# Soft-capped attention feeding a slot mixture of experts: casting loads, a second exponential tile per batch on VectorE, and three small jobs moved to the thin steps

## The chip, the cores and the metric

The kernel runs on one core of a Trainium2 chip. The metric is device time in microseconds (us), given as the median of several runs of the same compiled kernel. A profile is one further execution recorded by the hardware profiler, and its span is about 2 us shorter than the device time. The engines are PE (TensorE, matmuls), ACT (ScalarE), DVE (VectorE), POOL (GpSimd) and SP (which here only issues transfers). PEclk is the clock that the hardware granted to PE, as a fraction of full speed.

Ratios are computed as the mean time of one kernel's fast runs over that of the other's fast runs recorded with them, so they are not quite the ratio of the medians quoted beside them. A run is called slow when it is over 1.5% above the fastest run of the same kernel. The program runs on this one core alone.

## The reference, cut to what matters

```python
def _attn_ref(q, k, v, cap):                     # q, k, v: (8, 12, 448, 64)
    scores = scale * np.matmul(q, k.transpose(0, 1, 3, 2))
    scores = cap * np.tanh(scores / cap)          # cap = 30
    attn = np.exp(scores - max); attn /= attn.sum(-1)
    return np.matmul(attn, v)

def _moe_ref(x, phi, w1, w2):                    # x: (3584, 768), 32 slots, 8 experts
    logits = x @ phi
    d = softmax over tokens of logits; slot_input = d.T @ x
    slot_out = relu(slot_input @ w1) @ w2         # per expert
    c = softmax over slots of logits
    return c @ slot_out
```

Every score needs one tanh and one exponential. That is 8 x 12 x 448 x 448 scores, twice, and it is the bulk of the work.

## The kernel before

Attention is cut into 56 chunks of six score tiles (128 x 448 each), seven chunks per batch. I call one chunk's turn in the program a step and number the steps of a batch 0 to 6. In each step ACT does two tanh instructions (from PSUM, three tiles each) and one exponential over six tiles in place. Step 2 of each batch has no value products, and I call it the thin step. One tile per batch is taken from ACT: DVE computes its exponential by a polynomial, in three parts.

```python
def exp_chunk(j):
    exp_part(j, 1 if j in shared else 0, CH)       # ACT: six tiles, or five
shared = [j for j in range(NCH - 2) if j % 7 == 3 and j > 7] if cap < 80 else []

def poly_exp(j, part):                              # DVE: the sixth
    if part == 0:   ...                             # three tensor_scalar
    elif part == 1: ...                             # two scalar_tensor_tensor on SBUF operands
    else:           ...                             # two more, the last writes the tile

def cast(nm, Q):                                    # q or k of four heads: f32 to bf16, reordered
    dve.tensor_copy(t.rearrange("p c (h d) -> p h c d", h=2),
                    raws.pop((nm, Q)).rearrange("p h (c d) -> p h c d", d=DH))
    if Q > 1: load(nm, Q + 1)

def transp(nm, Q):
    for c in range(NT):
        pe.transpose(ps[:, c, :], src[:, c, :], ident)
    dve.tensor_copy(t, ps)

def e_transp(b):     # transposes of the combine weights, in the single buffer "T" of PSUM
    ps = psT.tile([P, 512], BF16, name="eps", tag="T")
    for g in (3, 0, 1, 2):
        pe.transpose(ps[:, GOFF[g]:GOFF[g] + P], e4s[b][:, g, :], ident)
    dve.tensor_copy(ET4..., ps...)
# e_norm(b): 4 matmuls "zps", then DVE adds "zacc";  e_sums: 7 matmuls "wps", then DVE "winv"
# x_transp(pr): 4 transposes "xps", then DVE copies "xT";  logits: 8 matmuls "lps", then DVE "lg"
# all of these use the one buffer "T" in turn

at(j + 1, "d", spare, 34 if b == 0 else 10)         # warm-up matmuls that compute nothing of use
...
at(j + 12, "d", e_transp, b)                        # step 5
at(j + 13, "d", e_norm, b)                          # step 6
at(j + 14, "d", e_sums, b // 2)                     # step 0, every other batch
for j in shared:
    for dj, slot, part in ((0, "a", 0), (0, "c", 1), (0, "d", 2)):
        at(j + dj, slot, poly_exp, j, part)
```

The slots of a step run in program order: tanh and exponential, value products of the first half, "a", scores, "b", value products of the second half, "c", scores, "d". In the timelines below each engine starts its instructions in this order.

The softmax here doesn't subtract the row's maximum and nothing guards it: scores larger than these inputs give would overflow.

## Time and profile before

| | before |
|---|---|
| time, median (range) | 318.18 us (317.34 to 319.43) |
| busy: PE / ACT / DVE / POOL | 269.4 / 281.3 / 193.7 / 106.5 us of a span of 314.8 |
| one batch, from one small exponential (L366) to the next | 32.56 us |
| ACT idle before tanh (L278) | 0.9 us in all |
| mean granted clock | 0.983 |

Read it like this: a busy share is an average, so it does not say what sets the time. The chain of waits and the idle column of ACT do. ACT hardly waits between about 7 and 268 us (busy 261.1 of 261.2 us), so in that stretch its work alone is the time. The prediction shows the lines.

### The profile page before, as it was taken

How to read it: one execution, taken by the hardware profiler on the slowest of the kernel's cores; microseconds unless marked ns; L12 is line 12 of the kernel's file. 1: busy time of each engine (PE TensorE's matmuls, PEld its weight loads, DVE VectorE, ACT ScalarE, POOL GpSimd, SP SyncE). 2: the span in 40 equal slices, each digit the busy share in tenths (PEclk: the TensorE clock that was granted, in tenths of full speed). 3: DMA queues.
4: the chain of work that ended last, by engine and by line, in shares of the span. 5: the costliest groups of instructions: out<-in, count | busy, mean ns of one | idle time of the engine just before them, and what ended most of it. 6: DMA issues, size and time to landing. Idle time of an engine off the chain costs nothing.

```text
span 314.8 us, 8844 instructions
## 1 busy us (share of the span) xinstructions
PE 269.4 (86%) x3804; PEld 191.0 (61%) x3804; DVE 193.7 (62%) x473; ACT 281.3 (89%) x208; POOL 106.5 (34%) x134
## 2 busy tenths in 40 slices
PE   7899898899889998898889989898889998998720
PEld 6667665667666665666666666666666677743400
DVE  3636565766586659575867587657766574327840
ACT  4999999999999999999999999999999999326730
POOL 2464342523543452354245416441732130200000
PEclk9999999999999999999999999999999999999985
DMA  8899999799999999999999999999999807898997
GB/s 223 267 234 238 291 244 269 159 231 256 235 210 231 266 237 207 254 220 266 194 225 269 221 264 190 242 235 266 209 232 254 214 14 207 290 393 301 389 411 314
DMA packets 57479, 77.68 MB, mean 247 GB/s; under 512 B 3809, under 2 KB 53601, under 8 KB 57441
## 3 DMA queue, kind: packets, MB, share of 16 engines
q0 software_dynamic: 30480, 25.22, 52.1%
q1 hardware_dynamic: 26672, 51.68, 48.1%
q8 instruction: 29, 0.48, 0.6%
q10 hardware_dynamic: 288, 0.23, 0.2%
q14 instruction: 10, 0.07, 0.1%
HBM read 91.32 MB, written 18.87 MB: 350 GB/s over the span
## 4 chain that ended last, share of the span: by engine, by line
ACT 67%; PE 20%; DVE 5%; issue 3%; DMA 2%; DVEq 0%; ACTq 0%
ACT ex L278 33%; ACT ex L282 32%; PE pv L318 5%; PE sc L269 3%; PE so_ps L676 2%; PE junk L506 2%; PE hp L649 2%; ACT ob L754 1%; PE op L702 1%; DMA kraw<-in_k_dram 1%; DVE xq L329 1%; PE op L745 1%; PE xps L344 1%; DMA out_dram<-obh 1%; DVE ob L752 1%
## 5 line engine op out<-in xcount | busy, mean ns | idle before, releaser
L278 ACT ACTIVATE ex<-sc 128x1344 bf16<-128x1344 f32 (+1 forms) x113 | 162.3, 1693 | 0.9 <-PE sc L269 0.8
L282 ACT ACTIVATE ex<-ex 128x2688 bf16<-128x2688 bf16 (+4 forms) x58 | 159.2, 2779 | 0.1
L318 PEld LDWEIGHTS <-ex 128*128 128x128 bf16 x1344 | 78.7, 97 | 21.5 <-DVE xq L329 17.8
L318 PE MATMUL pv<-vbd,ex 128*128 128x130 bf16 x1274 | 88.6, 220 | 2.6 <-ACT ex L282 0.7
L269 PE MATMUL sc<-qT,kT 64*64 64x448 bf16 x672 | 78.6, 358 | 8.2 <-ACT ex L278 7.9
L247 POOL CAST vbd<-vraw 64x896 bf16<-64x896 f32 x23 | 21.5, 936 | 103.6 <-PE pv L318 65.3
L269 PEld LDWEIGHTS <-kT 64*64 64x64 bf16 x672 | 27.3, 105 | 25.3 <-issue 7.5
L329 DVE TENSOR_TENSOR xq<-pv,rec 128x256 bf16<-128x256 f32 x91 | 38.6, 424 | 3.1
L328 DVE RECIPROCAL rec<-pv 128x4 f32<-128x4 f32 x91 | 16.5, 181 | 32.1 <-PE pv L318 31.2
L506 PEld LDWEIGHTS <-ones 128*128 128x128 bf16 x470 | 28.6, 100 | 11.6 <-DVE xq L329 8.0
L372 POOL COPY e<-E 128x512 bf16<-128x512 bf16 x9 | 7.2, 795 | 81.5 <-ACT E L366 49.6
L506 PE MATMUL junk<-ones 128*128 128x128 bf16 x433 | 31.4, 219 | 2.5 <-DVE xq L329 1.6
L239 DVE COPY kT<-kps 128x896 bf16<-128x896 bf16 x23 | 14.4, 625 | 24.6 <-PE kps L237 24.4
L109 POOL DMA_DIRECT2D w1b<-in_moe_w_dram x32 | 25.2, 791 | 0.0
L248 POOL CAST vbd<-vraw 64x896 bf16<-64x896 f32 x23 | 23.7, 1029 | 1.3
L346 DVE COPY xT<-xps 128x512 bf16<-128x512 bf16 x47 | 19.5, 415 | 3.2 <-PE xps L344 3.0
L344 PE MATMUL xps<-ident,xq 128*128 128x128 bf16 x188 | 18.1, 218 | 0.2 <-DVE zacc L383 0.2
L239 DVE COPY qT<-qps 128x896 bf16<-128x896 bf16 x23 | 14.2, 616 | 5.2 <-PE qps L237 5.2
L226 DVE CAST kbf<-kraw 128x896 bf16<-128x896 f32 x22 | 16.0, 728 | 1.3 <-DMA kraw<-in_k_dram 1.3
L237 PE MATMUL kps<-ident,kbf 128*128 128x128 bf16 x161 | 12.8, 219 | 4.2 <-DVE slacc L418 2.2
L237 PE MATMUL qps<-ident,qbf 128*128 128x128 bf16 x161 | 12.8, 219 | 3.2 <-DVE lg L360 2.7
L237 PEld LDWEIGHTS <-kbf 128*128 128x128 bf16 x161 | 10.0, 97 | 9.0 <-issue 8.3
(113 smaller groups left out, 255.5 us busy)
## 6 DMA issues: line engine op xcount, KB each, us to landing
w1b<-in_moe_w_dram POOLq DMA_DIRECT2D x32, 384.0 KB, 10.2
vraw<-in_v_dram SPq DMA_DIRECT2D x23, 448.0 KB, 6.6
qraw<-in_q_dram SPq DMA_DIRECT2D x22, 448.0 KB, 7.8
kraw<-in_k_dram SPq DMA_DIRECT2D x22, 448.0 KB, 6.0
w2d<-in_moe_w_dram POOLq DMA_DIRECT2D x20, 384.0 KB, 9.2
w2t<-w2d SPq DMA_DIRECT2D x20, 384.0 KB, 5.9
out_dram<-ob SPq DMA_DIRECT2D x8, 768.0 KB, 7.3
w2b<-in_moe_w_dram POOLq DMA_DIRECT2D x12, 384.0 KB, 9.9
```

What stands on the lines that cost most here:

```text
L109: pool.dma_start(out=w1b[e][:, js, fs], in_=w1r[:, e, js, fs])
L237: pe.transpose(ps[:, c, :], src[:, c, :], ident)
L239: dve.tensor_copy(t, ps)
L247: pool.tensor_copy(t[0:HP, :, :, 0:DH], raw[0:HP])
L248: pool.tensor_copy(t[HP:P, :, :, DH + 1:VW - 1], raw[HP:P])
L269: pe.matmul(sc[cs, u, 0:S], qkT["k", Q][r, c, cs], qkT["q", Q][r, :, cs], start=True, stop=True)
L278: act.activation(exs[j][:, half * CS + u0:half * CS + u1, :], sc[:, u0:u1, 0:S], ACT.Tanh, scale=qk_scale / cap)
L282: act.activation(exs[j][:, u0:u1, :], exs[j][:, u0:u1, :], ACT.Exp, scale=cap)
L318: pe.matmul(pvs[pr, half][:, n, 0:VW], exs[j][:, u, GOFF[g]:GOFF[g] + P], vbds[Q % 2][:, h, c, :], start=(c == 0 and n == 0), stop=(c == N ...
L329: dve.tensor_tensor(xq[Q][:, 2 * half:2 * half + 2, h * P:(h + 1) * P] .rearrange("p g (i d) -> p g i d", i=2), pv[:, :, :, 0:DH], rec.to_ ...
L344: pe.transpose(ps[:, g, :], xq[Q][:, g, h * P:(h + 1) * P], ident)
L506: pe.matmul(junk if home is None else home, ones, ones, start=True, stop=True)
```

## The change

The intent: give ACT less to do by moving a second tile per batch to DVE. To make room on DVE, q and k are cast to bf16 by the transfers, and the transfers are issued by POOL. The reordering that DVE's cast did on the way is given up, so each key or query transpose becomes two of 64 columns. To make room on PE in the dense steps, three small jobs go to steps 1 and 2, and warm-up matmuls are cut.

```diff
-    def cast(nm, Q):            # DVE cast of each q and k
+    def load(nm, Q):            # bf16 tiles, two buffers
+            (sp if nm == "v" else pool).dma_start(out=t, in_=quad_ap(nm, Q))
...
+            for h in range(2):
+                pe.transpose(ps[h * HP:h * HP + HP, c, :], src[:, h, c * DH:(c + 1) * DH], ident)
...
-    shared = [j for j in range(NCH - 2) if j % 7 == 3 and j > 7] if cap < 80 else []
+    shared = [j for j in range(NCH - 2) if j % 7 in (1, 3) and j > 7] if cap < 80 else []
...
-        at(j + 1, "d", spare, 34 if b == 0 else 10)
-        at(j + 2, "d" if b == 0 else "a", spare, 4 if b == 0 else 14)
+        at(j + 1, "d", spare, 34 if b == 0 else 6)
+        at(j + 2, "d" if b == 0 else "a", spare, 4 if b == 0 else 12)
...
-        at(j + 3, "d", spare, 10)
+        at(j + 3, "d", spare, 10 if b == 0 else 4)
...
-                at(j + 12, "d", e_transp, b)
-                at(j + 13, "d", e_norm, b)
+                at(j + 15, "d", e_transp, b)        # step 1
+                at(j + 16, "d", e_norm, b)          # step 2
             if b % 2:
-                at(j + 14, "d", e_sums, b // 2)
+                at(j + 16, "d", e_sums, b // 2)     # step 2
     for j in shared:
-        for dj, slot, part in ((0, "a", 0), (0, "c", 1), (0, "d", 2)):
-            at(j + dj, slot, poly_exp, j, part)
+        for slot, part in (("a", 0), ("c", 1)):
+            at(j, slot, poly_exp, j, part)
+        at(j + 1, "b" if j % 7 == 1 else "a", poly_exp, j, 2)
```

Cut: the first loads with their tiles, and the loads' new slots.

More of the change, by code (lines that the diff above doesn't have):

```diff
@@ L90 @@
     w1b = [wts.tile([P, NJ, F], BF16, name=f"w1b{e}", tag="w1", bufs=E)
-           for e in range(E - 1)]
+           for e in range(E - 2)]
     w2b = wts.tile([P, R2, D], BF16, name="w2b")
@@ L129 @@
     ld = att.enter_context(tc.tile_pool(name="ld", bufs=1))
-    cst = att.enter_context(tc.tile_pool(name="cst", bufs=1))
     ldv = att.enter_context(tc.tile_pool(name="ldv", bufs=1))
@@ L158, in raw_tile @@
     def raw_tile(nm):
-        return (ldv if nm == "v" else ld).tile([P, 2, S], F32, name=nm + "raw",
-                                               tag=nm + "raw")
+        if nm == "v":
+            return ldv.tile([P, 2, S], F32, name="vraw", tag="vraw")
+        return ld.tile([P, 2, S], BF16, name=nm + "b", tag=nm + "raw", bufs=2)
     def load(nm, Q):
@@ L164, in load @@
             t = raw_tile(nm)
-            sp.dma_start(out=t, in_=quad_ap(nm, Q))
+            (sp if nm == "v" else pool).dma_start(out=t, in_=quad_ap(nm, Q))
             raws[nm, Q] = t
     def load_first():
-        for nm in "qkv":
-            raws[nm, 0] = raw_tile(nm)
-        kc = raws["k", 0].rearrange("p h (c d) -> p h c d", d=DH)
+        for nm in "qk":
+            raws[nm, 0] = [ld.tile([P, S], F32, name=f"{nm}raw{h}", tag=nm + "raw", bufs=2)
+                           for h in range(2)]
+        raws["v", 0] = raw_tile("v")
+        kc = raws["k", 0][0].rearrange("p (c d) -> p c d", d=DH)
         kin = quad_ap("k", 0, 0).rearrange("p (c d) -> p c d", d=DH)
-        sp.dma_start(out=raws["q", 0][:, 0, :], in_=quad_ap("q", 0, 0))
+        sp.dma_start(out=raws["q", 0][0], in_=quad_ap("q", 0, 0))
         for c0, c1 in ((0, CS), (CS, NT)):
-            act.dma_start(out=kc[:, 0, c0:c1, :], in_=kin[:, c0:c1, :])
+            act.dma_start(out=kc[:, c0:c1, :], in_=kin[:, c0:c1, :])
         for nm in "kq":
-            sp.dma_start(out=raws[nm, 0][:, 1, :], in_=quad_ap(nm, 0, 1))
+            sp.dma_start(out=raws[nm, 0][1], in_=quad_ap(nm, 0, 1))
         t = wts.tile([P, 3, 2, S], F32, name="raw1", tag="w1", bufs=E)
+        t01 = wts.tile([P, 2, 2, NT, P], BF16, name="casts", tag="w1", bufs=E)
         for n, nm in enumerate("kqv"):
             raws[nm, 1] = t[:, n, :, :]
+            if nm != "v":
+                for Q in range(2):
+                    casts[nm, Q] = t01[:, n, Q, :, :]
             if nm == "v":
@@ L192, in first_pieces @@
                 copy(casts[nm, 0][:, c0:c1, cols],
-                     raws[nm, 0][:, h, c0 * DH:c1 * DH].rearrange("p (c d) -> p c d", d=DH))
+                     raws[nm, 0][h][:, c0 * DH:c1 * DH].rearrange("p (c d) -> p c d", d=DH))
             elif stage == "turn":
@@ L202, in first_half @@
             if h == 0:
-                casts[nm, 0] = cst.tile([P, NT, P], BF16, name=nm + "bf", tag=nm + "bf")
                 qkT[nm, 0] = qk.tile([P, NT, P], BF16, name=nm + "T", tag=nm + "T")
@@ L222, in first_half, with cast @@
                 load(nm, 2)
-    def cast(nm, Q):
-        t = cst.tile([P, NT, P], BF16, name=nm + "bf", tag=nm + "bf")
-        dve.tensor_copy(t.rearrange("p c (h d) -> p h c d", h=2),
-                        raws.pop((nm, Q)).rearrange("p h (c d) -> p h c d", d=DH))
-        casts[nm, Q] = t
-        if Q > 1:
-            load(nm, Q + 1)
+    def cast(nm):
+        dve.tensor_copy(casts[nm, 1].rearrange("p c (h d) -> p h c d", h=2),
+                        raws.pop((nm, 1)).rearrange("p h (c d) -> p h c d", d=DH))
     def transp(nm, Q):
-        src = casts.pop((nm, Q))
+        src = casts.pop((nm, Q)) if Q == 1 else raws.pop((nm, Q))
         home = (psV, "pv") if (nm, Q) == ("k", 1) else (psT, "T")
@@ L236, in transp @@
         for c in range(NT):
-            pe.transpose(ps[:, c, :], src[:, c, :], ident)
+            if Q == 1:
+                pe.transpose(ps[:, c, :], src[:, c, :], ident)
+                continue
+            for h in range(2):
+                pe.transpose(ps[h * HP:h * HP + HP, c, :], src[:, h, c * DH:(c + 1) * DH], ident)
         t = qk.tile([P, NT, P], BF16, name=nm + "T", tag=nm + "T")
@@ L441, in quad_in @@
         if 0 < Q < NQ:
-            at(*cast_k, cast, "k", Q)
-            at(*cast_q, cast, "q", Q)
+            for nm, when in (("k", cast_k), ("q", cast_q)):
+                at(*when, *((cast, nm) if Q == 1 else (load, nm, Q + 1)))
             at(*k_in, transp, "k", Q)
@@ L453 @@
             quad_in(3 * b + 1, (j - 1, "b"), (j, "a"), (j - 1, "d"), (j, "c"), (j + 1, "d"))
-        quad_in(3 * b + 2, (j + 1, "c"), (j + 2, "c"), (j + 2, "b"), (j + 2, "d"),
+        quad_in(3 * b + 2, (j, "d"), (j + 1, "c"), (j + 2, "b"), (j + 2, "d"),
                 (j + 4, "d"))
-        quad_in(3 * b + 3, (j + 4, "a"), (j + 5, "a"), (j + 4, "d"), (j + 5, "c"),
+        quad_in(3 * b + 3, (j + 4, "a"), (j + 5, "a"), (j + 3, "d"), (j + 5, "c"),
                 (j + 6, "d"))
         p = 6 * b
-        at(j + 1, "d", spare, 34 if b == 0 else 10)
-        at(j + 2, "d" if b == 0 else "a", spare, 4 if b == 0 else 14)
+        at(j + 1, "d", spare, 34 if b == 0 else 6)
+        at(j + 2, "d" if b == 0 else "a", spare, 4 if b == 0 else 12)
         if b:
             at(j + 2, "c", spare, 8)
-        at(j + 3, "d", spare, 10)
+        at(j + 3, "d", spare, 10 if b == 0 else 4)
         at(j + 4, "a", x_transp, p)
@@ L476 @@
             if b < B - 2:
-                at(j + 12, "d", e_transp, b)
-            if b < B - 2:
-                at(j + 13, "d", e_norm, b)
+                at(j + 15, "d", e_transp, b)
+                at(j + 16, "d", e_norm, b)
             if b % 2:
-                at(j + 14, "d", e_sums, b // 2)
+                at(j + 16, "d", e_sums, b // 2)
     for j in shared:
-        for dj, slot, part in ((0, "a", 0), (0, "c", 1), (0, "d", 2)):
-            at(j + dj, slot, poly_exp, j, part)
+        for slot, part in (("a", 0), ("c", 1)):
+            at(j, slot, poly_exp, j, part)
+        at(j + 1, "b" if j % 7 == 1 else "a", poly_exp, j, 2)
     for n, job in enumerate(wjobs):
```

## The prediction

> **What bounds the kernel now.** I read the share of each engine first, then the chain that ended last, then the groups by shape, then one steady batch in order of time. From the page, the chain:
>
> ```profile
> ACT 67%; PE 20%; DVE 5%; issue 3%; DMA 2%; DVEq 0%; ACTq 0%
> ```
>
> Two thirds of the span hang on ScalarE (ACT). The groups by shape (busy us, mean ns, then idle time before them) say which instructions, and that nothing holds them up:
>
> ```profile
> L278 ACT ACTIVATE ex<-sc 128x1344 bf16<-128x1344 f32 x111 | 161.1, 1710 | 0.0
> L282 ACT ACTIVATE ex<-ex 128x2688 bf16<-128x2688 bf16 x48 | 137.7, 2869 | 0.1
> ...
> L282 ACT ACTIVATE ex<-ex 128x2240 bf16<-128x2240 bf16 x7 | 18.1, 2579 | 0.0
> ...
> L226 DVE CAST kbf<-kraw 128x896 bf16<-128x896 f32 x22 | 16.0, 728 | 1.3 <-DMA kraw<-in_k_dram 1.3
> L226 DVE CAST qbf<-qraw 128x896 bf16<-128x896 f32 x22 | 14.5, 660 | 0.0
> ```
>
> The tanh (L278) and exponential (L282) instructions overlap, so their means exceed what each adds. The timeline of ACT gives the cost by start times (start us, us, engine, line):
>
> ```profile
> 114.58 2.79 ACT L282 ACTIVATE ex<-ex 128x2688 bf16<-128x2688 bf16 x1
> 116.92 2.82 ACT L278 ACTIVATE ex<-sc 128x1344 bf16<-128x1344 f32 x2
> ...
> 121.59 0.67 ACT L366 ACTIVATE E<-lg 128x128 bf16<-128x128 f32 x1
> ...
> 124.13 2.45 ACT L282 ACTIVATE ex<-ex 128x2240 bf16<-128x2240 bf16 x1
> 126.09 1.67 ACT L278 ACTIVATE ex<-sc 128x1344 bf16<-128x1344 f32 x1
> ```
>
> A full exponential of six tiles takes 116.92 - 114.58 = 2.34 us, one of five tiles (the sixth done by VectorE) 126.09 - 124.13 = 1.96 us. Two tanh take 2.35 us, so a step (one chunk of six tiles) is 4.69 us, and a batch of seven steps runs from 121.59 to the next small exponential at 154.15: 32.56 us, with ACT busy all of it. From 6.8 to about 268 us this engine sets the time; the remaining 47 us (expert layers, output) are other code and the change does not touch them.
>
> TensorE (PE) is a close second. Two batches by windows (busy us and count by engine):
>
> ```profile
> 96.00:128.56 32.56, 29.20 (x425) 21.21 (x423) 22.27 (x56) 32.56 (x24) 13.52 (x17) 1.00 1.06 230
> 128.56:161.12 32.56, 28.96 (x418) 21.12 (x416) 22.01 (x55) 32.56 (x24) 13.29 (x17) 1.00 1.06 225
> ```
>
> PE is idle only some 3.4 us of 32.56, and most of that is round trips to VectorE (DVE) through single buffers, not spare time.
>
> [...] The weight transfers of this kernel do so already: their median from issue to landing is 10.2 us for w1, against 6.0 and 7.8 us for the plain k and q loads.[...] six 448-column score matmuls, two column halves, take 0.57 us[...].
>
> **The change, part by part.**
>
> *Exponential tiles.* Shared chunks were those with j mod 7 = 3, 10 to 52: seven. Those with j mod 7 = 1 from 8 to 50 are added: seven more. ACT loses 7 x 0.373 = 2.6 us. This lies on the path, so the ideal is 318.17 - 2.6 = 315.6 us. DVE gains per tile the seven polynomial instructions, 382 + 394 + 394 + 613 + 626 + 666 + 872 ns = 3.95 us, 27.6 us in all.
>
> *Casts.* 44 casts leave DVE: 22 x 728 + 22 x 660 ns = 30.5 us. DVE's load thus stays near 190 us (62%): the casts pay for the polynomials. They were not on the path, so removing them alone gives nothing.
>
> *Transfers.* 44 loads of 448 KB move from SP's queue to POOL's, landing as bf16. POOL's issue costs about 0.77 us each (row of the weight issues): 34 us more on an engine busy 106 of 315 us, mostly waiting. HBM reads are unchanged. Landing grows from 6 to 8 us towards the 10 us of the weights, but the loads now have two buffers and are issued about 11 to 14 us ahead of their transposes (by my reading of POOL's order: after a value cast at 127.3, for a transpose near 139). I expect them hidden.
>
> *Key and query transposes.* Without the reordering cast, each 128x128 transpose becomes two of 64 columns in the two column halves: 44 x 7 = 308 more matmuls. Before, the first quad did exactly this form:
>
> ```profile
> 7.85 0.55 PE L196 MATMUL ps<-ident,kbf 128*64 128x128 bf16 x7
> 8.24 0.55 PE L196 MATMUL ps<-ident,qbf 128*64 128x128 bf16 x7
> ```
>
> Seven take 8.24 - 7.85 = 0.39 us, 55 ns each, the same as full ones. There all seven were in one half. If two halves run together as the score matmuls do, the extra is near zero; if not, it is 6 x 7 x 55 ns = 2.3 us per batch.[...]
>
> *Fillers and the thin step.* Twelve fewer warm-up matmuls per batch from the second on: 12 x 55 = 0.66 us back. The weights' transposes, normalizer and sums, each with a DVE round trip of 0.2 to 0.5 us, move from the dense steps to those with fewer value products. Key transposes of one quad move one step earlier. This evens PE out.
>
> *Sum for PE per batch.* Free before: about 1 us of waiting for ACT (7.9 us over 7.5 batches), plus 0.66 us of fillers removed, plus about 0.3 us of round trips hidden, less the 0.37 us by which ACT gets shorter: 1.6 us. Needed: 0 to 2.3 us[...]. So in the parallel case ACT stays the bound; in the serial case PE overshoots ACT's new period by 0.7 to 1.3 us per batch, that is 5 to 9 us over seven batches on top of 315.6.
>
> **Rivals.**
> 1. *PE becomes the bound* because the half transposes are serial. For: PE is already 90% busy in a batch, and the second score group of a dense step ends only 0.7 to 0.8 us before ACT needs it (98.62 against 99.4 us). Against: the concurrent score matmuls, and the trimmed fillers, which look balanced by hand. It would make 320 to 325 us.
> 2. *Late loads on POOL's queue.* For: [...]the weights are 768 KB of reading each, and one took 16.0 us to land; POOL also waits up to 6.6 us on value products before it can issue. Against: the lead of 11 to 14 us and unchanged bytes. If each batch lost 0.5 to 1 us: 319 to 323 us.
> 3. *Polynomials in DVE's way*: parts of 1.2, 1.2 and 1.5 us ahead of a reciprocal that frees the single value buffer. For: PE's weight loads waited 17.8 us on that line before. Against: the third part was moved a step later, and casts of 0.6 to 0.7 us leave the same queue. At most a few tenths per batch: 316 to 318 us.
> 4. *More gain than 2.6 us*: nothing speaks for it, as ACT had 1 us of idle time in all and the tail is unchanged. Beyond 314 us would need a faster start or tail.
>
> **How the range follows.** I choose the parallel case with two in three, small stalls of about 0.4 us in all on top of 315.6: 316.0. The serial or late-load cases, one in three, lift the upper end; the spread of the runs before (317.34 to 318.18) sets the lower. Range 314.5 to 320.0 us. Faster by over 2% means under 311.8, which ACT's arithmetic excludes: 0.02. Slower by over 2% means over 324.5[...]: 0.06. Within 2%: 0.92.
>
> **What would show it.** ACT's five-tile exponentials count 14, six-tile ones 41; the batch from one small exponential to the next is 32.2 us; ACT idle before L278 stays under 2 us. The transposes show in pairs: 14 in 0.45 to 0.6 us rather than 0.94. No wait of a transpose on a k or q load. DVE busy near 190 us. I am wrong if ACT waits on score matmuls, PE on these loads, or if the pairs are serial and the batch exceeds 32.6 us.

Some passages of the prediction are cut, at the marks, because they rested on rules or figures that no trace or run of this case shows. The forecast came to 318.17 - 7 x 0.373 = 315.6 us, plus stalls of about 0.4 us, so 316.0 us. The passage that first gave 0.373 us is cut, but the trace before shows the figure: from its start to the next start on ACT a six-tile exponential takes 2.333 us and a five-tile one 1.960 us, by the median. In the sum for PE one term is cut: an estimate of about 0.1 us for each change between groups of different tile shape, 0.6 us per batch. With it PE needed up to 2.3 + 0.6 = 2.9 us against the 1.6 us free, which is the overshoot of 1.3 us per batch, or 9 us in all. Without it the overshoot is at most 0.7 us, or 5 us in all. The 0.06 for slower by over 2% rested on that cut term.

"Do so" of the weight transfers means that they cast while they land and that POOL issues them. That the score matmuls run in pairs is measured in the trace before: the six start two by two, within 0.03 us of each other, most often at 0, 0.21 and 0.40 us, and a group takes 0.57 to 0.76 us. One after another they would take about 1.2 us. That is an estimate from the 55 ns of a 128-column transpose: 6 x 448 / 128 x 55 ns.

## The result and the profile after

The changed kernel takes 335.63 us (333.34 to 337.21, four runs, all fast) against 318.18 us. The ratio is 1.054, with a 95% interval of 1.047 to 1.061. The prediction was 316.0 us with a range of 314.5 to 320.0, and 0.06 for slower by over 2%. It was wrong.

From the page of the changed kernel, the chain that ended last; then, from its groups by shape, ACT's instructions (now at L286 and L290) and the second instruction of the polynomial's second part (L309):

```profile
ACT 48%; PE 31%; DVE 14%; issue 2%; DMA 1%; DVEq 0%; ACTq 0%
```

```profile
L286 ACT ACTIVATE ex<-sc 128x1344 bf16<-128x1344 f32 x111 | 140.4, 1341 | 17.0 <-PE pv L326 13.0 <-PE sc L277 3.9
L290 ACT ACTIVATE ex<-ex 128x2688 bf16<-128x2688 bf16 x41 | 102.5, 2499 | 0.1
L290 ACT ACTIVATE ex<-ex 128x2240 bf16<-128x2240 bf16 x14 | 29.9, 2136 | 0.0
...
L309 DVE SCALAR_TENSOR_TENSOR xp<-xp,xm 128x448 f32<-128x448 f32 x14 | 13.1, 938 | 0.5
```

The 14 exponentials of five tiles are there as planned, but ACT now stands idle 17.0 us before its tanh. Its share of the chain fell from 67% to 48%, and PE's and DVE's rose to 31% and 14%. So ACT got less work and then waited for PE. The releaser "PE pv" (13.0 us of the 17.0) is to be taken as it stands. A tanh writes one of four buffers named ex in turn, and the value products (pv) of the chunk four steps back still read that buffer. At the wait of 2.73 us shown below, the last value product that reads the buffer ends at 124.90 us and the tanh starts at 124.94, while its scores had ended at 124.10.

Where it goes is seen in four batches by windows, each from one small exponential to the next (length, then busy us and count of PE, PEld, DVE, ACT, POOL, then the granted clock, the DMA share and GB/s):

```profile
88.18:121.91 33.73, 30.10 (x439) 21.39 (x440) 20.90 (x55) 32.80 (x23) 18.01 (x22) 0.93 1.08 193
121.91:157.84 35.93, 32.69 (x457) 23.11 (x454) 22.25 (x57) 32.51 (x23) 16.74 (x21) 0.88 1.00 172
157.84:195.83 37.99, 34.11 (x451) 23.76 (x449) 22.90 (x57) 32.62 (x23) 17.63 (x22) 0.81 0.99 166
195.83:231.24 35.41, 31.79 (x465) 22.15 (x464) 22.92 (x60) 32.30 (x23) 17.50 (x22) 0.96 0.98 172
```

The batches are 33.7 to 38.0 us long instead of 32.2, and the granted clock, 1.00 in these batches before, is down to 0.81. The number of matmuls differs little from batch to batch, yet PE's busy time grows, because each takes longer: 68.4 to 75.6 ns of busy time for one, against 29.08 us over 457 = 63.6 ns in a batch of number 2 below, at a clock of 1.00.

One thin step shows the cause. First PE's timeline (start, us, engine, line, what; idle time before it in brackets):

```profile
110.84 0.40 PE L399 MATMUL eps<-ident,e 128*128 128x128 bf16 x4
111.21 0.51 PE L514 MATMUL junk<-ones 128*128 128x128 bf16 x6
113.31 0.38 PE L352 MATMUL xps<-ident,xq 128*128 128x128 bf16 x4 [1.58 <-DVE ET L400]
113.53 1.44 PE L514 MATMUL junk<-ones 128*128 128x128 bf16 x12
114.90 1.33 PE L277 MATMUL sc<-qT,kT 64*64 64x448 bf16 x6
```

Then DVE at the same time:

```profile
111.07 0.61 DVE L308 SCALAR_TENSOR_TENSOR xp<-xm 128x448 f32<-128x448 f32 x1
111.72 1.23 DVE L309 SCALAR_TENSOR_TENSOR xp<-xp,xm 128x448 f32<-128x448 f32 x1
112.88 0.38 DVE L400 COPY ET<-eps 128x448 bf16<-128x448 bf16 x1
```

The weights' transposes (eps) end at 111.24, but the copy that frees the single PSUM buffer starts only at 112.88. It stands in DVE's queue behind the second part of the new tile's polynomial. The x transposes (xps) need that buffer. No matmul that stands after them in the program begins before them, the fillers included, and so PE stands still for 1.58 us. The granted clock (third number from the end) then falls, from 1.00 in the window before these:

```profile
112.00:114.00 2.00, 0.69 (x9) 0.69 (x9) 1.53 (x3) 2.00 (x3) 1.94 (x3) 0.89 1.24 204
114.00:116.00 2.00, 2.00 (x16) 1.05 (x13) 0.15 (x1) 2.00 (x2) 2.00 (x3) 0.50 1.23 228
116.00:118.00 2.00, 2.00 (x29) 1.42 (x28) 0.85 (x2) 1.71 (x2) 0.02 (x1) 0.76 1.13 269
```

The next score group takes 1.33 us where 0.76 was usual, and ACT runs dry for 2.73 us:

```profile
124.94 2.47 ACT L286 ACTIVATE ex<-sc 128x1344 bf16<-128x1344 f32 x2 [2.73 <-PE pv L326]
```

Over the run the x transposes waited 10.9 us in six batches, up to 2.3 us each. Before the change they did not wait for that copy at all; the logits (lps) waited for it 2.9 us in six batches, up to 0.5 us each.

L309 itself takes 1.23 us where its twin in step 3 takes 0.62. All seven in step 1 took 1.23 to 1.26 us, and each overlaps a value cast on POOL that took 1.23 to 1.24 instead of 0.96 us. L309 is so up to 0.63 us longer. The instruction before it (L308, of the same kind) took up to 1.27 us instead of 0.61 in the same places. In the six waits the two together took 1.84 to 2.52 us instead of 1.24, which adds up to 5.6 of the 10.9 us. So about half of the wait is the extra length of these two. That the casts beside them cause it is my reading of the overlap; no run took it away by itself.

### The profile page after: what moved, and what is told of

Same layout as the page of the kernel before. It is cut to its first block, busy times and chain, and to the rows that moved or that the text cites. A ratio compares the mean times of both kernels' runs of the same rounds, so it can differ in the third digit from the quotient of the medians.

```text
span 331.6 us, 9262 instructions
## 1 busy us (share of the span) xinstructions
PE 284.4 (86%) x4028; PEld 197.1 (59%) x4028; DVE 192.6 (58%) x478; ACT 279.9 (84%) x208; POOL 136.8 (41%) x178
## 4 chain that ended last, share of the span: by engine, by line
ACT 48%; PE 31%; DVE 14%; issue 2%; DMA 1%; DVEq 0%; ACTq 0%
ACT ex L286 24%; ACT ex L290 22%; PE pv L326 8%; PE sc L277 5%; PE junk L514 3%; DVE xp L309 2%; DVE xq L337 2%; PE so_ps L684 2%; PE hp L657 2%; PE kps L245 2%; DVE xp L308 2%; PE qps L245 2%; PE op L753 1%; ACT ob L762 1%; PE xps L352 1%
## 5 line engine op out<-in xcount | busy, mean ns | idle before, releaser
L286 ACT ACTIVATE ex<-sc 128x1344 bf16<-128x1344 f32 (+1 forms) x113 | 141.6, 1330 | 17.8 <-PE pv L326 13.0
L290 ACT ACTIVATE ex<-ex 128x2688 bf16<-128x2688 bf16 (+4 forms) x58 | 135.0, 2333 | 0.1
L326 PE MATMUL pv<-vbd,ex 128*128 128x130 bf16 x1274 | 94.7, 227 | 4.1 <-ACT ex L290 2.4
L326 PEld LDWEIGHTS <-ex 128*128 128x128 bf16 x1344 | 82.3, 101 | 26.5 <-DVE xq L337 12.9
L277 PE MATMUL sc<-qT,kT 64*64 64x448 bf16 x672 | 83.4, 375 | 3.9 <-ACT ex L286 2.3
L514 PEld LDWEIGHTS <-ones 128*128 128x128 bf16 x386 | 25.5, 106 | 7.2 <-issue 2.8
L352 PE MATMUL xps<-ident,xq 128*128 128x128 bf16 x188 | 18.1, 219 | 11.6 <-DVE ET L400 10.9
L352 PEld LDWEIGHTS <-xq 128*128 128x128 bf16 x188 | 12.9, 97 | 13.0 <-issue 13.0
L167 POOL DMA_DIRECT2D qb<-in_q_dram x22 | 16.2, 738 | 3.5 <-DVE kT L206 3.4
L245 PE MATMUL qps<-ident,qb 128*64 128x128 bf16 x308 | 14.3, 238 | 2.9 <-DVE lg L368 2.9
L245 PEld LDWEIGHTS <-kb 128*64 128x64 bf16 x308 | 10.8, 122 | 9.5 <-issue 9.5
```

Source lines behind the costliest of these rows:

```text
L245: pe.transpose(ps[h * HP:h * HP + HP, c, :], src[:, h, c * DH:(c + 1) * DH], ident)
L277: pe.matmul(sc[cs, u, 0:S], qkT["k", Q][r, c, cs], qkT["q", Q][r, :, cs], start=True, stop=True)
L286: act.activation(exs[j][:, half * CS + u0:half * CS + u1, :], sc[:, u0:u1, 0:S], ACT.Tanh, scale=qk_scale / cap)
L290: act.activation(exs[j][:, u0:u1, :], exs[j][:, u0:u1, :], ACT.Exp, scale=cap)
L326: pe.matmul(pvs[pr, half][:, n, 0:VW], exs[j][:, u, GOFF[g]:GOFF[g] + P], vbds[Q % 2][:, h, c, :], start=(c == 0 and n == 0), stop=(c == N ...
L352: pe.transpose(ps[:, g, :], xq[Q][:, g, h * P:(h + 1) * P], ident)
```

## The experiments

My first theory (A): the late copy stops PE, the clock falls, and ACT runs dry. Rival B: the transfers or the doubled transposes are too much. Rival C: too few warm-up matmuls. The first four kernels ran together, each an edit of the changed kernel.

| run | median (range), us | ratio of fast runs [95%] | clocks of the runs |
|---|---|---|---|
| changed kernel | 335.63 (333.34 to 337.21) | 1.054 [1.047, 1.061] | 0.913 to 0.929 |
| 1 copy first | 321.73 (316.4 to 326.9) | 0.996 [0.989, 1.003] | 0.932, 0.947; 0.979, 0.980 |
| 2 all three jobs back | 315.76 (314.18 to 317.35) | 0.994 [0.987, 1.0005] | 0.982 to 0.987 |
| 3 more fillers | 328.42 (324.44 to 333.56) | 1.023 [1.015, 1.030] | 0.939 to 0.974 |
| 4 old fillers | 333.74 (326.83 to 342.05) | one fast run only | 0.912 to 0.959 |
| 5 fillers in the chain | 316.81 (315.6 to 318.12) | 0.996 [0.991, 1.001] | 0.982 to 0.987 |
| 6 only transposes back | 323.96 (320.06 to 326.36) | 1.014 [1.007, 1.022] | 0.938 to 0.962 |
| 7 jobs back, one tile | 317.51 (317.16 to 317.74) | 0.9985 [0.994, 1.003] | 0.979 to 0.986 |
| 8 kernel before, two tiles | 327.12 (326.24 to 327.37) | 1.028 [1.024, 1.032] | 0.979 to 0.984 |
| 9 number 2 again | 314.57 (314.33 to 315.62) | 0.991 [0.986, 0.995] | 0.978 to 0.985 |

The kernel before had medians of 317.40 (runs 1 to 4), 317.99 (5 to 8, on another chip) and 317.31 us (9). Of the seven runs behind the last figure, six are those of runs 1 to 4 and one is new (316.67 us). The changed kernel itself was not run again beside the experiments. All results were correct.

**1. The copy ahead of the polynomial.**

```diff
-        for slot, part in (("a", 0), ("c", 1)):
+        for slot, part in (("a", 0), ("d" if j % 7 == 1 else "c", 1)):
```

> Edit to the changed kernel: for the new tile (chunks with j mod 7 = 1) the second polynomial part is queued on VectorE after the copy of the moved weights' transpose instead of ahead of it. Nothing else. Theory A (the copy waits behind the polynomial, TensorE stands idle 1.5 to 2.3 us before the x transposes, its clock is then halved, and ScalarE runs dry for 2.6 to 3.1 us): the wait of those transposes falls from 10.9 us in six to under 4 us, granted clock back to at least 0.975, time 315.5 to 319 us. Rival B (the transfers on GpSimd's queue, or the doubled transposes, load TensorE and the queues too much): at least 330 us, as these are untouched. Rival C (fewer warm-up matmuls alone let the clock fall): clock stays near 0.93 and time above 328 us.

The wait of the x transposes for the weights' copy is gone from the list of waits. But the runs fell on two levels: 316.4 and 316.6 us with clocks of 0.979 and 0.980, and twice 326.9 us with 0.932 and 0.947. The upper two count as slow, and the profile is of one of them. In it every second batch is 36.2 to 36.4 us long and the others 32.2. So the first cause is real, but there is another, in every second batch. Every second batch is where the sums (e_sums) run. I changed the theory to A2: two culprits. The evidence for the second is not taken from this run but from number 6, whose profile is of a fast run.

**2. All three jobs back in their old steps.**

```diff
-                at(j + 15, "d", e_transp, b)
-                at(j + 16, "d", e_norm, b)
+                at(j + 12, "d", e_transp, b)
+                at(j + 13, "d", e_norm, b)
-                at(j + 16, "d", e_sums, b // 2)
+                at(j + 14, "d", e_sums, b // 2)
```

> Edit to the changed kernel: the weights' transposes, the normalizer and the sums go back to the steps where they stood before (5, 6 and 0 of each batch); two tiles on VectorE, cast transfers and split transposes stay. Theory A: no copy is left behind the polynomial at the thin step, so clock at least 0.975 and time 315.5 to 319 us. If the dense steps had been full without the move, ScalarE would wait a few tenths per batch and the time would be 318 to 322 us. Rival B: at least 330 us. Rival C: clock near 0.93, above 328 us.

Four fast runs, 314.2 to 317.4 us, clock 0.982 or more. Its batches by windows:

```profile
88.28:120.46 32.18, 29.08 (x457) 20.73 (x453) 21.88 (x58) 32.18 (x24) 18.00 (x22) 1.00 1.11 196
120.46:152.64 32.18, 28.94 (x449) 20.58 (x444) 21.67 (x56) 32.18 (x24) 16.97 (x21) 1.00 1.12 194
```

Every batch is 32.18 us, the figure that the prediction drew from ACT's arithmetic. Two tiles, casting loads, split transposes and cut fillers are all still in. So rivals B and C fall: without the move of the three jobs the loss is not there. Between this profile and that of the changed kernel the span differs by 331.6 - 312.4 = 19.2 us. Five batches of the latter (33.73, 35.93, 37.99, 35.41 and, up to the next small exponential at 265.34, 34.10 us) account for 177.16 - 5 x 32.18 = 16.3 us of it; a last wait of ACT at the following thin step (2.70 us at 265.6) makes up most of the rest.

**3. More fillers where PE waited.**

```diff
-        at(j + 1, "d", spare, 34 if b == 0 else 6)
+        at(j + 1, "d", spare, 34 if b == 0 else 40)
```

> Edit to the changed kernel: 40 instead of 6 warm-up matmuls between the weights' transposes and the wait for their copy, so TensorE is busy (34 x 55 ns = 1.9 us more) while it waits; order on VectorE unchanged. This separates the wait from the clock. If the halved clock is what turns the wait into the loss (theory A with the clock as amplifier): clock at least 0.975, time 316 to 321 us though the copy is as late as before. If the wait itself is the loss and the clock only a sign: time stays above 329 us. Rival B: at least 330 us.

A miss for both readings. The wait for the copy is down to 0.2 us. Yet even the two fast runs took 324.4 and 325.5 us, with clocks of 0.974 and 0.967. I had overlooked that the second culprit is untouched here. In the profile (of a slow run) ACT waits 1.13 us at 121.6 although the clock is 1.00 throughout 112 to 124 us. There the copy came later too (24.94 us after the batch's small exponential, against 24.70 in the changed kernel) and PE still waited 0.24 us for it. So PE was late in spite of the fillers, and the sums followed. So a late PE costs some time at full clock too, and this run does not separate wait and clock. Better evidence stands in the profile of the changed kernel, step by step. In two of its six thin steps with a wait, the x transposes waited 1.87 us (until 80.93) and 1.82 us (until 223.76), the clock stayed at 1.00 in the ten microseconds after, and ACT's next wait was 0.25 and 0.20 us. In the other four they waited 1.52 to 2.27 us, the clock fell to 0.50, and ACT lost 3.4 to 4.7 us each time. So most of the loss needs the fall of the clock.

**4. The fillers as before the change** (10, 14 and 10 instead of 6, 12 and 4).

> Edit to the changed kernel: the three numbers of warm-up matmuls that the change cut (6, 12, 4 per batch) are put back to 10, 14, 10. Theory A: four more behind the weights' transposes cover 4 x 55 ns = 0.2 us of a wait of 1.5 to 2.3 us, so the clock still falls in some batches: clock 0.92 to 0.96, time 326 to 337 us. Rival C (the cut fillers are the cause): clock at least 0.975 and time 316 to 320 us.

326.8 to 342.1 us, clock 0.912 to 0.959; the x transposes still waited 9.4 us (in the profile, which is of a slow run). One run lies above the expected range, and the single fast run took 326.83 us, far from the 316 to 320 that rival C called for. Rival C falls: the cut fillers were not the cause.

**5. Fillers inside the chain of the thin step,** on top of the edit of number 1.

```diff
                 at(j + 16, "d", e_norm, b)
+                at(j + 16, "d", spare, 10)
                 at(j + 16, "d", e_sums, b // 2)
+                at(j + 16, "d", spare, 6)
...
+            if Q % 3 == 2 and Q > 3:
+                at(*q_in, spare, 7)
             at(*q_in, transp, "q", Q)
```

> The first experiment's order (the copy ahead of the second polynomial part) plus warm-up matmuls between the normalizer (10), the sums (6), the logits (7) and the query transposes of the thin step, to cover the three waits of 0.56, 0.29 and 0.38 us there; the moved parts stay where the change put them and the DVE round trips stay. Theory A2 (a second culprit: this chain of round trips without fillers lowers the clock in the batches with sums, 36.3 instead of 32.2 us each): clock at least 0.975 in all runs, every batch 32.2 us, time 315 to 318 us with no run above 319. Rival D (the chain is simply too long for TensorE in the thin step, clock or not): still 322 to 327 us in some runs and periods of 35 us or more in odd batches.

All four runs are fast, 315.6 to 318.1 us, clock 0.982 to 0.987; batches are 32.17 to 32.64 us long. From PE's timeline of this run:

```profile
115.66 0.25 PE L387 MATMUL zps<-ones,e 128*128 128x1 bf16 x4
115.77 0.72 PE L518 MATMUL junk<-ones 128*128 128x128 bf16 x10
116.47 0.31 PE L409 MATMUL wps<-ones,ET 128*128 128x1 bf16 x7
116.64 0.49 PE L518 MATMUL junk<-ones 128*128 128x128 bf16 x6
...
117.81 0.58 PE L245 MATMUL qps<-ident,qb 128*64 128x128 bf16 x14
```

The transposes (qps) begin 2.15 us after zps, as in the next run without fillers (117.50 - 115.33 = 2.17). PE has the same round trips to sit out; it only has matmuls to do meanwhile, and the clock holds. So rival D falls: the chain is not too long, it is too empty. This is the separation that number 3 failed to give. The fast runs of number 1, without these fillers, were as fast (316.4 and 316.6 us). What the fillers take away is the fall of the clock: by the mean clocks, two of four runs there had it, none of four here, and all four of number 6, whose lowest time is 320.06 us.

**6. Only the weights' transposes back,** normalizer and sums left in the thin step.

> The changed kernel with only the weights' transposes back at step 5; normalizer and sums stay in the thin step, polynomial order as changed. Theory A2: the first culprit is gone, the second remains, so it behaves like the first experiment: two levels, about 316 us in runs without a fall of the clock and 323 to 328 us with falls in batches that have sums; no wait for the transposes' copy before x transposes. If the normalizer and sums were harmless: all runs 315 to 318 us. If the transposes were not the first culprit: above 330 us.

320.1 to 326.4 us, a single spread rather than the two levels that I expected; three of the four runs are fast, the ratio is 1.014. The profile is of a fast run (323.75 us). Its batches between 87.98 and 256.74 us are 32.18, 36.18, 32.18, 36.04 and 32.18 us long: only those with sums suffer. From PE's timeline, then the clock:

```profile
115.33 0.25 PE L387 MATMUL zps<-ones,e 128*128 128x1 bf16 x4
116.14 0.31 PE L409 MATMUL wps<-ones,ET 128*128 128x1 bf16 x7 [0.56 <-DVE zacc L391]
116.75 0.37 PE L363 MATMUL lps<-phib,xT 128*128 128x32 bf16 x8 [0.30 <-DVE winv L410]
117.50 0.96 PE L245 MATMUL qps<-ident,qb 128*64 128x128 bf16 x14 [0.38 <-DVE lg L368]
118.39 1.70 PE L326 MATMUL pv<-vbd,ex 128*128 128x130 bf16 x14
```

```profile
116.00:118.00 2.00, 1.19 (x26) 1.13 (x27) 0.58 (x4) 2.00 (x3) 0.00 (x0) 0.66 1.23 215
118.00:120.00 2.00, 2.00 (x23) 1.65 (x19) 0.62 (x1) 2.00 (x2) 0.00 (x0) 0.50 1.24 206
```

Three round trips to DVE through the one buffer follow each other, with 0.56, 0.30 and 0.38 us of idle PE. By windows the clock reads 1.00 up to 116.6 us and 0.50 from there on, so it falls during the second of them. It stays halved until about 126.9 us, for some ten microseconds, and fourteen value products take 1.70 us instead of the 0.98 of number 5. In a batch without sums the middle trip is missing and the clock stays at 1.00 (windows from 146 to 152 us). Here too the first wait is made longer by the polynomial: the third part (0.62 + 0.62 us) stands on DVE's queue ahead of zacc. So the two culprits have roughly equal weight, as far as medians of spread runs on two chips tell: from the changed kernel to this one the medians fall by 335.63 - 323.96 = 11.7 us, and from this one to number 2 by 323.96 - 315.76 = 8.2 us.

**7. Jobs back, one tile per batch** (number 2 with `j % 7 == 3` alone).

> The second experiment (transposes, normalizer and sums back) with only one tile per batch on VectorE as before the change; cast transfers and split transposes stay. This is the transfers' part alone. Theory: ScalarE is again the bound with its old work, 32.55 us per batch, time 316.8 to 319 us, ratio to before 0.998 to 1.004. Then two tiles are worth 2.6 us at this place. Rival B (the transfers or split transposes cost TensorE time on the path): 320 us or more.

317.51 us, all runs within 0.6 us, ratio 0.9985. The batches are 32.55 us long, as before the change, with DVE busy 163.9 us. The casting loads and the split transposes by themselves neither gain nor lose.

**8. The kernel before with two tiles, nothing else.**

```diff
-    shared = [j for j in range(NCH - 2) if j % 7 == 3 and j > 7] if cap < 80 else []
+    shared = [j for j in range(NCH - 2) if j % 7 in (1, 3) and j > 7] if cap < 80 else []
-        for dj, slot, part in ((0, "a", 0), (0, "c", 1), (0, "d", 2)):
-            at(j + dj, slot, poly_exp, j, part)
+        for slot, part in (("a", 0), ("c", 1)):
+            at(j, slot, poly_exp, j, part)
+        at(j + 1, "b" if j % 7 == 1 else "a", poly_exp, j, 2)
```

> The kernel before with two tiles per batch on VectorE, in the changed order of the polynomial parts, and nothing else: casts stay on VectorE, loads on SP, moved parts at their old places. VectorE is then busy about 194 + 28 = 222 us. If VectorE has the room (it was busy 22 of 32.6 us per batch): 314.5 to 317 us like the second experiment, and cast transfers were not needed. If the casts have to go to make room, as the change supposes: norms come late, TensorE waits for the value buffer, clock below 0.975 or ScalarE idle, and 318 to 326 us.

327.12 us, ratio 1.028, outside the two expectations by a hair (I had said up to 326). DVE is busy 221.0 us, as expected: 68% of the span, so by the average there is room. But the queue is what counts:

```profile
117.58 0.55 PE L237 MATMUL kps<-ident,kbf 128*128 128x128 bf16 x7 [0.57 <-DVE xT L346]
...
120.77 0.55 PE L237 MATMUL qps<-ident,qbf 128*128 128x128 bf16 x7 [1.21 <-DVE lg L360]
```

The query transposes wait 1.21 us for the logits sum (lg), which stands on DVE's queue behind the third polynomial part and a cast of 0.62 us. Over the run they waited 8.5 us so, in seven places. The clock stays at 1.00 in these batches, so this is the price of DVE's queue alone: a batch takes 34.0 to 34.3 us. So, with the polynomial's parts at these places, the casts do have to leave DVE for the second tile to pay; no other placing was tried.

**9. Number 2 once more, with more rounds.**

> The second experiment's kernel once more, unaltered, with more rounds, because its gain of 0.6% had an interval that touched 1 and its runs fell on two levels (314.2 and 317.2 us). If ScalarE's seven times 0.373 us are all there is: 315 to 316 us, ratio to before 0.990 to 0.996 with an interval below 1, and batches of 32.2 us again. If the second level is as frequent as the first, the mean gain is half of that and the interval may still touch 1.

314.57 us, all six runs fast, ratio 0.991 with an interval of 0.986 to 0.995. It beats the kernel before (317.31 us), by 0.9%, and the changed kernel. The batches are 32.16 to 32.18 us again. The median is a little below the 315 that I expected. The second level of number 2 (317.2 us) did not return; why it was there is open, as no profile of such a run was taken.

## Why the prediction was wrong, point by point

- **ACT bounds the kernel, and a second tile is worth 7 x 0.373 = 2.6 us (2.333 - 1.960 us by start times, seven times): right.** The batch became 32.18 us when nothing else was in the way (numbers 2 and 9). Number 9 gained 317.31 - 314.57 = 2.7 us.
- **Casts pay for polynomials on DVE: right.** DVE was busy 192.6 us after, 193.7 before. Without the casts' removal the second tile costs 9 us (number 8). The prediction only said that the loads are equal; it did not see how much hangs on it.
- **Loads on POOL's queue are hidden (rival 2 falls): right.** They landed in 7.7 us (k) and 7.5 us (q) by the median, 14.5 at most, and no wait of PE on them is in the list. Number 7 confirms it. POOL's two value casts took 0.93 and 0.96 us by the median, before and after.
- **Two half transposes run together (rival 1 falls): right.** Fourteen take 0.58 us at full clock, where seven whole ones took 0.55. The estimate of about 0.1 us for a change of tile shape has a like in the trace before. From the start of seven whole transposes (tiles of 128*128) to the next group it was 0.39 us by the median where value products (also 128*128) followed and 0.49 where scores (64*64) did; from the start of fourteen half ones it is 0.51 us by the median in both cases. Why it is so is not shown. Number 7 shows that this is not on the path. One reading behind the prediction was off: six score matmuls take 0.57 us only in the groups in which four of them start together. Most groups take 0.76 us, as three pairs about 0.2 us apart (starts at 0, 0.21 and 0.40 us); that pairs run together holds.
- **"The weights' transposes, normalizer and sums ... move from the dense steps to those with fewer value products. This evens PE out": this step failed.** It counted PE's matmuls and not the waits between them. A thin step is thin in matmuls, so nothing hides a round trip there. In the dense steps, scores and value products do. In place of an even PE, the runs showed PE idle for 1.5 to 2.3 us before the x transposes of six thin steps and for 0.56, 0.30 and 0.38 us in the chain with the sums, and batches of up to 38.0 us. With the three jobs back in their old steps every batch took 32.18 us (number 2).
- **Rival 3, polynomials in DVE's way, was the right mechanism with the wrong size and place.** The prediction gave it "at most a few tenths per batch" and looked at the value buffer. It was the transposes' buffer, and the wait was 1.5 to 2.3 us. The prediction had the pieces (1.2 us parts in step 1, a copy moved to step 1) and did not lay them in one queue in order.
- **The granted clock was not in the sum at all.** The prediction called fillers warm-up matmuls and counted their removal as a gain of 0.66 us per batch, without asking what PE's clock does when PE pauses. That term measured: the two levels of number 1, 316.5 and 326.9 us, and, in the changed kernel, 3.4 to 4.7 us of ACT after each of four thin steps against 0.20 and 0.25 us after the two with a like wait and full clock.

Why did the same wait lower the clock in one batch and not in another? The trace of the changed kernel says more than I first saw. By windows the clock changed at 113.56, 116.98, 120.39, 123.80, 151.11, 164.76, 188.66, 198.90 and 256.92 us. The times between are 1, 1, 1, 8, 4, 7, 3 and 17 times 3.413 us. If one counts on from them in stretches of that length, the six waits for the copy fall into two kinds. Four had at least 1.52 us within one stretch (PE was busy 42 to 54% of it), and the clock fell at the end of that stretch each time. Two were cut by the end of a stretch into pieces of at most 1.50 us, and it did not fall. For example, the wait of 1.87 us is cut at 79.43 us, and the one of 1.58 us lies whole between 110.15 and 113.56. So in these six waits the fall went with where a wait lay on these stretches, and the kernel does not set that. It may be why equal kernels differ from run to run (number 1), which is not shown.

What stays open: what exactly lowers the clock. From 116.98 to 120.39 us PE was busy 2.22 us and the clock fell at the end; from 79.43 to 82.84 us it was busy only 1.91 us and the clock did not fall. Six waits of one profile give no rule.

## What to carry to other kernels

When a job is moved to a step with little other work, move its waits into the account too: find what stands ahead of each of its instructions in the other engine's queue, and what the waiting engine has to do meanwhile. Six to ten useless matmuls in a gap can be worth more than the time they take: with them the clock was 0.982 to 0.987 in all four runs (number 5), without them 0.932 and 0.947 in two of four (number 1). There they fitted inside the waits (2.15 us from zps to qps with them, 2.17 without); what longer ones cost there was not run. Judge an engine's room by its queue at the place in question, not by its busy share.
